# Loads of stored low parts moved to another queue, tile twiddles copied three at a time, operand sums woven in more tightly

## The chip, the core and the metric

The kernel runs on one core of a Trainium2 chip. A core has five engines with an instruction queue each: TensorE (PE, matrix products; PEld is its weight load), VectorE (DVE), ScalarE (ACT), GpSimd (POOL) and SyncE (SP). In this kernel SP and POOL mostly issue DMAs. The metric is device time in microseconds (us), the median over runs. Before the change it is 1392.01 us, over three runs from 1389.22 to 1394.37.

## The reference

The output mixes two branches of the same input `x` (2048 tokens of 576 features) with a gate per token:

```
g = sigmoid((x * gate_w).sum(-1, keepdims=True))
a = irfft2(rfft2(x) * (w_r + 1j * w_i))            # spectral branch, over (2048, 576)
b = (gelu(x @ w_gate) * (x @ w_up)) @ w_down        # 576 -> 4608 -> 576
return g * a + (1 - g) * b
```

All of it is in float32.

## The kernel before

**The dense branch sets TensorE's order.** The 4608 hidden features are 36 tiles of 128 (`j`), the tokens two halves of 1024 (`p`), each of two blocks of 512 (`tb`). A float32 operand is split into a high part of type fp32r and the low rest, and a product is three matmuls: high by high, low by high, high by low. The weights of `j` lie in `gu[j % 3]` (gate and up) and `dn[j % 4]` (down), as `[:, 0]` high and `[:, 1]` low, made from the loaded `raws`. `chain` runs one gate or up product (lines 761 to 768), `hidden` a gate and an up chain and the product of the two, `down_mm` (line 821) the down product. A step `n` of the main loop is two `hidden` calls and four downs of the step before. Its downs are scaled by ScalarE into one of four tiles `stg` (line 846) and added to a DRAM tensor `yd` by an accumulating DMA from POOL's queue (line 834).

**Low parts are kept.** In the first token half (`p` = 0) VectorE subtracts the low parts, and for the first eight `j` they are also stored to DRAM tensors `lo`. In the second half, `lower` (line 730) loads these eight back instead of computing them: `gu<-lo` of 640 KB and `dn<-lo` of 288 KB, both by line 733 in SP's queue. From there on (`products`) seven products per pair of tiles replace eight, for which `operands` and `last_operand` make sums of parts of `x`.

**The spectral branch lies beside it.** It is a mixed-radix transform on VectorE and ScalarE: rows (`forward_rows`), tiles of columns (`first_tiles`, `columns`, `last_tiles`), then back (`inverse_rows`). `columns` also uses TensorE for 64-point products (`product`, line 274, six matmuls per pair of columns) on high and low operands in `colm`: `xh`, `xl` before the filter, `yh`, `yl` after it, where the low one is VectorE's line 267. Corner values move between halves of the partitions by small DMAs in SP's queue (`cns<-til`, `til<-cns`).

**What sets the order.** All instructions are written out in one order by hand. TensorE's chains call `gap()` some 800 times; in each gap the spectral generator gives its next instructions while a credit (VectorE time against TensorE time, `RATE`) is above zero, and `yield None` ends a gap. `columns` has a side generator `beside`, which runs the butterflies and the twiddles of the tiles. Each engine's queue runs in order, so an instruction that waits holds up all behind it on its engine.

**Twiddles.** A tile twiddle turns three complex units. For each, ScalarE copies the unit scaled by a sine into a scratch tile (line 113), and two VectorE instructions combine it in place (lines 127 and 129); for a quarter turn ScalarE does the combination alone (lines 124, 125). `_twiddles` runs the copies `ahead` units in front, which in `beside` is one, with two scratch tiles; the third copy waits until the first scratch is read.

Of the kernel before, what the change touches and what calls it, by code (L numbers as in the profile page):

```python
# [12 lines left out]
AF = mybir.ActivationFunctionType  # L13
# [90 lines left out]
def _twiddles(eng, act, unit, real, imag, places, tmps, sgn, cost):  # L104

    todo = list(places)
    ahead = min(2, len(tmps) - 1)

    def scaled(i):
        if i < len(todo):  # L110
            at, n = todo[i]
            s = 1.0 if n == 4 else sgn * math.sin(math.pi * n / 8)
            act.activation(tmps[i % len(tmps)][0], unit(*at), AF.Copy, scale=s)

    yield None
    for i in range(ahead):
        scaled(i)
    yield None
    for i, (at, n) in enumerate(todo):
        scaled(i + ahead)  # L120
        c, (_, tr, ti) = math.cos(math.pi * n / 8), tmps[i % len(tmps)]
        xr, xi = real(*at), imag(*at)
        if n == 4:
            act.activation(xr, ti, AF.Copy, scale=-float(sgn))
            act.activation(xi, tr, AF.Copy, scale=float(sgn))
            continue
        eng.scalar_tensor_tensor(xr, xr, c, ti, op0=ALU.mult, op1=ALU.subtract)
        yield cost
        eng.scalar_tensor_tensor(xi, xi, c, tr, op0=ALU.mult, op1=ALU.add)
        yield cost  # L130


def _block_of_token():
# [25 lines left out]
def _build(nc, tc, a):  # L159
    with ExitStack() as ctx:  # L160
# [69 lines left out]
        def columns():  # L230
# [62 lines left out]
            def beside():  # L293

                more = gates()
                tmps = [flat[:, SW * i:SW * (i + 1)] for i in (1, 2)]
                for d in range(1, 4):
                    yield from tile_twiddles(d, TAKEN, -1, tmps)
                    yield from four(d, TAKEN, sp, -1)
                    made[0] = d  # L300
                for d in range(3):
                    while gone[0] < (4 * d + 5) * STEP + 5:
                        yield next(more, None)
                    yield from four(d, range(4), sp, 1)
                yield from more
                for k in (1, 2):
                    yield from tile_twiddles(k, LEFT, 1, tmps)
# [19 lines left out]
            for kb in range(18):  # L327
                on, was = kb < 16, 1 <= kb < 17
                if kb < 16:
                    z, (w0, w1) = two(Z[kb]), ww[kb % 2]  # L330
                    zr, zi = z[:, 0], z[:, 1]

                def filter_start():
                    vec.tensor_tensor(zi, v[0][:, :NK], zr, ALU.subtract)
                    vec.tensor_tensor(zr, v[0][:, :NK], zr, ALU.add)

                def swap():
                    act.activation(vs2[0:64], z[64:128], AF.Copy, scale=-1.0)
                    copy(vs2[64:128], z[0:64])

                def filter_end():
                    vec.tensor_tensor(z, z, two(vs), ALU.add)
                    vec.tensor_tensor(vs2[:, 0], zr, zi, ALU.add)
                    vec.tensor_tensor(vs2[:, 1], zr, zi, ALU.subtract)

                for g in range(STEP):
                    if g == 0:
                        while kb % 4 == 2 and kb < 14 and made[0] < kb // 4 + 1:
                            credit[0] -= next(side[0])
                        if on:  # L350
                            v = product(0, kb, xh, xl)
                            load_ww(kb + 1)
                            corner(kb + 2, 0, False)
                        if was:
                            copy(yh, vs)
                    elif g == 1:
                        if on:
                            copy(zr, v[1][:, :NK])
                        if kb + 1 < 16:
                            copy(xh2, two(Z[kb + 1]))  # L360
                        corner(kb - 2, 2, True)
                    elif g == 2:
                        if on:
                            filter_start()
                        if was:
                            low(yl, vs, yh)
                    elif g == 3:
                        if on:
                            swap()
                            corner(kb + 2, 0, True)  # L370
                        if kb + 1 < 16:
                            low(xl2, two(Z[kb + 1]), xh2)
                    elif g == 4:
                        if was:
                            w = product(1, kb - 1, yh, yl)
                            for c in range(2):
                                copy(two(Z[kb - 1])[:, c], w[c][:, :NK])
                        if on:
                            vec.tensor_tensor(z, z, two(w0), ALU.mult)
                            vec.tensor_tensor(vs, vs, w1, ALU.mult)  # L380
                    elif g == 5:
                        if on:
                            filter_end()
                        if was:
                            corner(kb - 1, 2, False)
                    if kb == 17 and g > 4:
                        break
                    credit[0] -= 5.45 / STEP if on else 0.0
                    gone[0] = kb * STEP + g
                    yield None  # L390
# [22 lines left out]

        def tile_twiddles(k, at, sgn, tmps):

            tmps = [(x, x[:, 0:NK], x[:, NK:]) for x in tmps]
            places = [((k, at[o]), o * k) for o in range(1, 4)]
            yield from _twiddles(vec, act, lambda d, e: T[:, d, e], lambda d, e: T[:, d, e, re],
                                 lambda d, e: T[:, d, e, im], places, tmps, sgn, 0.5)

        def last_tiles():

            rows = rows_tile()
            sp = rows[:, 0:4 * SW].rearrange("p (e k) -> p e k", e=4)
            yield from tile_twiddles(3, LEFT, 1, [rows[:, SW * i:SW * (i + 1)] for i in range(4, 8)])
            yield None
            yield from _butterfly(vec, lambda i: T[:, i], lambda i: T[:, i, :, re], lambda i: T[:, i, :, im],
                                  range(4), sp, 1, (2.6, 1.35))
# [132 lines left out]

        def woven(main, other):

            n, free = 0, 0
            for v in main:
                yield v
                n += 1
                if n % 2 == 0 and reloaded[0] and count[0] > free:
                    w = next(other, 0.0)
                    if w is None:  # L570
                        free = count[0]
# [158 lines left out]
        def lower(key, g, r, cost):  # L730
            j, i = key[1], key[0] == "dn"
            if NT <= j < NT + 2 * FIRST:
                nc.sync.dma_start(f(g[:, 1]), lows[j - NT][i])
                return

            def run():
# [574 lines left out]
```

## Time and profile before

| | before |
|---|---|
| median of three runs | 1392.01 us |
| the profiled execution's own time | 1387.69 us |
| its span, first to last instruction | 1385.8 us |
| mean granted TensorE clock | 0.998 |
| TensorE busy | 1366.2 us, 99% |
| VectorE busy | 1119.8 us, 81% |
| ScalarE busy | 703.8 us, 51% |
| GpSimd busy | 266.2 us, 19% |

The page divides the span by engines, lists which group of instructions waited for what, and follows a chain of waits back from the end. `gu<-lo` reads "written `gu`, read `lo`"; L762 is line 762. A number in brackets behind an instruction is the time that its engine was idle before it, and what ended that. TensorE works throughout, so the stretches in which it is idle are the ones that matter.

### The profile page before, as it was taken

The page shows a single profiled execution, that of the slowest core. Times are in us where ns is not written, and L with a number is a line of the kernel's source. Part 1 is how long each engine was busy: PE and PEld are TensorE (multiplying, and loading weights), DVE is VectorE, ACT ScalarE, POOL GpSimd, SP SyncE. Part 2 cuts the span into 40 slices and gives each one's busy share as a digit, 9 for nine tenths or more (in the row PEclk, how much of TensorE's full clock was granted, in tenths as well). Part 3 has the DMA queues.
Part 4 walks back from the last instruction along what each step waited for, and adds up shares of the span by engine and source line. Part 5 has one row for each costly group of instructions (what it writes and reads, how often), then busy time and mean ns, then how long its engine had stood idle before and what let it go on. Part 6 is the DMA issues. An engine that isn't in the chain of part 4 may idle for free.

```text
span 1385.8 us, 20125 instructions
## 1 busy us (share of the span) xinstructions
PE 1366.2 (99%) x7490; PEld 1206.0 (87%) x7490; DVE 1119.8 (81%) x1649; ACT 703.8 (51%) x1095; POOL 266.2 (19%) x326
## 2 busy tenths in 40 slices
PE   9999999999999999999998999999999999999998
PEld 7888888888888888888887888888888888888887
DVE  6989999998877876999979873587777777777776
ACT  5553434355656665444464549445555555555552
POOL 0021111121222211111141023212111121111110
PEclk9999999999999999999999999999999999999999
DMA  9577765668899996556789588767667667776776
GB/s 341 198 179 153 180 116 97 123 117 185 213 272 260 247 235 121 99 112 124 148 185 253 197 171 189 141 128 131 130 129 130 130 130 131 127 129 130 131 154 172
DMA packets 102226, 226.65 MB, mean 164 GB/s; under 512 B 12400, under 2 KB 22640, under 8 KB 101744
## 3 DMA queue, kind: packets, MB, share of 16 engines
q0 software_dynamic: 45248, 92.56, 44.0%
q1 hardware_dynamic: 56880, 132.81, 30.2%
q8 instruction: 59, 0.97, 0.3%
q14 instruction: 39, 0.32, 0.1%
HBM read 118.56 MB, written 99.61 MB: 157 GB/s over the span
## 4 chain that ended last, share of the span: by engine, by line
PE 58%; DMA 1%; DVE 1%; ACT 0%; issue 0%; SPq 0%; DVEq 0%; ACTq 0%
PE pdn L821 20%; PE pgu L1016 4%; PE pgu L1018 4%; PE pgu L1017 4%; PE px L1016 3%; PE px L1018 3%; PE px L1017 3%; PE pgu L762 2%; PE pgu L763 2%; PE pgu L761 2%; PE px L761 2%; PE px L763 2%; PE px L762 2%; PE pgu L1019 2%; PE px L1019 1%; DMA gu<-lo 1%
## 5 line engine op out<-in xcount | busy, mean ns | idle before, releaser
L834 POOL DMA_DIRECT2D yd<-stg x264 | 230.1, 872 | 1028.3 <-ACT stg L846 975.3
L846 ACT ACTIVATE stg<-pdn,omg 128x576 f32<-128x576 f32 x272 | 201.9, 742 | 380.2 <-PE pdn L821 282.1
L821 PEld LDWEIGHTS pdn<-dn,hb 128*128 128x128 f32 x2760 | 382.0, 188 | 11.6 <-DVE raws L875 0.5
L821 PE MATMUL pdn<-dn,hb 128*128 128x288 f32 x2760 | 389.9, 295 | 0.2 <-DVE raws L875 0.2
L762 PE MATMUL pgu<-xhi,gu 128*128 128x512 f32 x440 | 172.5, 392 | 4.2 <-DMA gu<-lo 3.9
L761 PE MATMUL pgu<-xhi,gu 128*128 128x512 f32 x440 | 172.6, 392 | 1.1 <-ACT gl L799 1.1
L763 PE MATMUL pgu<-xlo,gu 128*128 128x512 f32 x440 | 172.1, 391 | 0.0
L213 ACT ACTIVATE gu<-raws 128x1280 fp32r<-128x1280 f32 (+3 forms) x84 | 86.4, 1029 | 38.8 <-PE px L767 28.3
L762 PEld LDWEIGHTS pgu<-xhi,gu 128*128 128x128 f32 x440 | 82.9, 189 | 19.7 <-DMA gu<-lo 4.4
L761 PE MATMUL px<-xhi,gu 128*128 128x512 f32 x256 | 100.0, 390 | 0.0
L763 PE MATMUL px<-xlo,gu 128*128 128x512 f32 x256 | 99.8, 390 | 0.0
L762 PE MATMUL px<-xhi,gu 128*128 128x512 f32 x256 | 99.7, 389 | 0.0
L763 PEld LDWEIGHTS pgu<-xlo,gu 128*128 128x128 f32 x440 | 83.0, 189 | 18.1
L761 PEld LDWEIGHTS pgu<-xhi,gu 128*128 128x128 f32 x440 | 83.0, 189 | 16.3 <-ACT gl L799 1.5
L821 PEld LDWEIGHTS pdn<-dn,gu 128*128 128x128 f32 x672 | 92.2, 188 | 2.1
L821 PE MATMUL pdn<-dn,gu 128*128 128x288 f32 x672 | 93.5, 295 | 0.0
L807 DVE TENSOR_TENSOR hb<-gl,hb 128x512 fp32r<-128x512 f32 x88 | 60.4, 687 | 38.0 <-ACT hb L213 37.9
L799 ACT ACTIVATE gl<-pgu 128x512 f32<-128x512 f32 x55 | 32.8, 596 | 92.3 <-PE pgu L768 85.8
L1034 DVE TENSOR_TENSOR xraw<-xraw 128x512 f32<-128x512 f32 x56 | 38.8, 693 | 31.2 <-ACT xraw L1042 30.7
L1051 DVE TENSOR_TENSOR gl<-gl,pgu 128x512 f32<-128x512 f32 x56 | 38.3, 684 | 27.8 <-PE pgu L1019 27.8
L763 PEld LDWEIGHTS px<-xlo,gu 128*128 128x128 f32 x256 | 48.1, 188 | 10.4
L213 ACT ACTIVATE hb<-gl 128x512 fp32r<-128x512 f32 x88 | 54.9, 624 | 3.3 <-DVE gl L803 3.3
(220 smaller groups left out, 2659.7 us busy)
## 6 DMA issues: line engine op xcount, KB each, us to landing
yd<-stg POOLq DMA_DIRECT2D x264, 288.0 KB, 5.1
raws<-wgu SPq DMA_DIRECT2D x42, 640.0 KB, 5.5
raws<-wd SPq DMA_DIRECT2D x72, 288.0 KB, 3.1
quads<-ws SPq DMA_DIRECT2D x24, 384.0 KB, 4.5
colm<-col POOLq DMA_DIRECT2D x32, 256.0 KB, 6.3
raws<-ws SPq DMA_DIRECT2D x21, 384.0 KB, 4.3
lo<-gu SPq DMA_DIRECT2D x8, 640.0 KB, 4.5
gu<-lo SPq DMA_DIRECT2D x8, 640.0 KB, 6.1
```

The costliest lines, as they stand in the source:

```text
L213: act.activation(o, i, AF.Copy)
L761: pe.matmul(ps, w[:, 0, k, c], xhi[tb][:, k], start=k == 0, stop=False)
L762: pe.matmul(ps, w[:, 1, k, c], xhi[tb][:, k], start=False, stop=False)
L763: pe.matmul(ps, w[:, 0, k, c], xlo[tb][:, k], start=False, stop=False)
L807: vec.tensor_tensor(h[:, 1], g, f(h[:, 0]), ALU.subtract)
L821: pe.matmul(ps[half], h[:, l, c], d[:, q, half * HD:(half + 1) * HD], start=part == 0 and n == 0, stop=part == 1 and n == 2)
L834: pl.dma_start(yd[u], o, accum_op=ALU.add)
L846: put(u, lambda o: act.activation(o.rearrange("p (c k) -> p c k", c=2), v[:, :, 0:HD], AF.Copy, scale=omg[:, u:u + 1]), i == 0)
L1016: pe.matmul(ps, hi[:, c], xh[:, t], start=t == 0, stop=False)
L1017: pe.matmul(ps, lo[:, c], xh[:, t], start=False, stop=False)
L1018: pe.matmul(ps, hi[:, c], xl[:, t], start=False, stop=False)
L1019: pe.matmul(ps, w[:, 512 + P * s:512 + P * (s + 1)], xt, start=False, stop=True)
```

## The change

The loads of the eight kept low parts go from SP's queue to POOL's (`lower`). Tile twiddles get a function of their own, `_three_twiddles`: it makes all three scaled copies in one gap, into three scratch tiles, ends two gaps, and then gives the VectorE instructions. `beside` gets its third scratch tile from a free part of `tmp`; `last_tiles` uses three of its four. The row twiddles keep `_twiddles`. A catch-up loop in `columns` accepts that the side generator ends a gap. `woven`, which gave one instruction of `operands` after every second row instruction, gives one after each.

```diff
+def _three_twiddles(eng, act, units, powers, tmps, sgn, cost):
+    yield None
+    for (x, _, _), n, (t, _, _) in zip(units, powers, tmps):
+        act.activation(t, x, AF.Copy, scale=1.0 if n == 4 else sgn * math.sin(math.pi * n / 8))
+    yield None
+    yield None
+    for (_, xr, xi), n, (_, tr, ti) in zip(units, powers, tmps):
+        c = math.cos(math.pi * n / 8)
+        for o, t, op, s in ((xr, ti, ALU.subtract, -float(sgn)), (xi, tr, ALU.add, float(sgn))):
+            if n == 4:
+                act.activation(o, t, AF.Copy, scale=s)
+            else:
+                eng.scalar_tensor_tensor(o, o, c, t, op0=ALU.mult, op1=op)
+                yield cost
...
-                tmps = [flat[:, SW * i:SW * (i + 1)] for i in (1, 2)]
+                tmps = [flat[:, SW * i:SW * (i + 1)] for i in (1, 2)] + [tmp[:, 3 * SW:4 * SW]]
...
-                            credit[0] -= next(side[0])
+                            credit[0] -= next(side[0]) or 0.0
...
         def tile_twiddles(k, at, sgn, tmps):
-            tmps = [(x, x[:, 0:NK], x[:, NK:]) for x in tmps]
-            places = [((k, at[o]), o * k) for o in range(1, 4)]
-            yield from _twiddles(vec, act, lambda d, e: T[:, d, e], lambda d, e: T[:, d, e, re],
-                                 lambda d, e: T[:, d, e, im], places, tmps, sgn, 0.5)
+            parts = [(x, x[:, 0:NK], x[:, NK:]) for x in tmps]
+            units = [(T[:, k, at[o]], T[:, k, at[o], re], T[:, k, at[o], im]) for o in range(1, 4)]
+            yield from _three_twiddles(vec, act, units, [o * k for o in range(1, 4)], parts, sgn, 0.5)
...
-            yield from tile_twiddles(3, LEFT, 1, [rows[:, SW * i:SW * (i + 1)] for i in range(4, 8)])
+            yield from tile_twiddles(3, LEFT, 1, [rows[:, SW * i:SW * (i + 1)] for i in range(4, 7)])
...
         def woven(main, other):
-            n, free = 0, 0
+            free = 0
             for v in main:
                 yield v
-                n += 1
-                if n % 2 == 0 and reloaded[0] and count[0] > free:
+                if reloaded[0] and count[0] > free:
                     w = next(other, 0.0)
...
             if NT <= j < NT + 2 * FIRST:
-                nc.sync.dma_start(f(g[:, 1]), lows[j - NT][i])
+                pl.dma_start(f(g[:, 1]), lows[j - NT][i])
                 return
```

The change adds lines, so line numbers of the changed kernel below are 15 to 17 higher: 733 becomes 748, 267 becomes 284, 607 becomes 622, 803 becomes 818.

The first place is the load of the low parts of `gu_71` for `j` = 37, the second tile of the second token half. Before, it stood in SP's queue, where `xt` is the input that is loaded again for the second half:

```order
L1177 DMA xraw<-xt 128x512 x2
L711 DMA raws<-wgu 128x1280
L712 DMA raws<-wd 128x576
L1177 DMA xraw<-xt 128x512 x2
L733 DMA gu_71<-lo_1280_115 128x1280
L1177 DMA xraw<-xt 128x512
```

Now it stands in POOL's queue, between the additions of the finished first-half spectral tiles (`yd<-til`):

```order
L622 DMA yd_99<-til 128x576
L748 DMA dn_73<-lo_576_114 128x576
L622 DMA yd_100<-til 128x576
L622 DMA yd_101<-til 128x576
L622 DMA yd_102<-til 128x576
L622 DMA yd_103<-til 128x576
L748 DMA gu_71<-lo_1280_115 128x1280
L622 DMA yd_104<-til 128x576
```

The load no longer stands behind four input loads and two weight loads, but behind seven of the eight accumulating DMAs of POOL.

The second place is VectorE at the start of `columns`, where the second tile is twiddled (L127, L129 before, L146 now) and the first low operand `xl` is made (L267 before, L284 now, `colm<-til,colm`). Before:

```order
L100 TENSOR_TENSOR til<-xraw,til 128x580 x2
L127 SCALAR_TENSOR_TENSOR til<-til,xraw 128x290
L129 SCALAR_TENSOR_TENSOR til<-til,xraw 128x290
L127 SCALAR_TENSOR_TENSOR til<-til,xraw 128x290
L129 SCALAR_TENSOR_TENSOR til<-til,xraw 128x290
L92 TENSOR_TENSOR xraw<-til 128x580
L92 TENSOR_TENSOR til<-til 128x580
L807 TENSOR_TENSOR hb_78<-gl_82,hb_78 128x512
L737 TENSOR_TENSOR dn_75<-raws,dn_75 128x576
L267 TENSOR_TENSOR colm<-til,colm 128x580
```

Now:

```order
L100 TENSOR_TENSOR til<-xraw,til 128x580 x2
L822 TENSOR_TENSOR hb_78<-gl_82,hb_78 128x512
L752 TENSOR_TENSOR dn_75<-raws,dn_75 128x576
L284 TENSOR_TENSOR colm<-til,colm 128x580
L146 SCALAR_TENSOR_TENSOR til<-til,xraw 128x290 x2
L146 SCALAR_TENSOR_TENSOR til<-til,tmp 128x290 x2
```

The low operand has moved ahead of the four twiddle instructions and of the two butterfly instructions behind them.

The third place is VectorE at the end of `columns`, where the last low operand `yl` is made (`colm<-tmp,colm`) while the last tile is twiddled. Before:

```order
L344 TENSOR_TENSOR tmp<-til 128x290
L803 TENSOR_TENSOR gl_82<-gl_82,pgu 128x512
L127 SCALAR_TENSOR_TENSOR til<-til,xraw 128x290
L129 SCALAR_TENSOR_TENSOR til<-til,xraw 128x290
L127 SCALAR_TENSOR_TENSOR til<-til,xraw 128x290
L129 SCALAR_TENSOR_TENSOR til<-til,xraw 128x290
L267 TENSOR_TENSOR colm<-tmp,colm 128x580
```

Now:

```order
L361 TENSOR_TENSOR tmp<-til 128x290
L818 TENSOR_TENSOR gl_82<-gl_82,pgu 128x512
L284 TENSOR_TENSOR colm<-tmp,colm 128x580
L146 SCALAR_TENSOR_TENSOR til<-til,xraw 128x290 x2
L146 SCALAR_TENSOR_TENSOR til<-til,tmp 128x290 x2
```

Here too the low operand has passed the four twiddle instructions.

## The prediction

> **What bounds the kernel now.** I read the page's busy times first.
>
> ```profile
> PE 1366.2 (99%) x7490; PEld 1206.0 (87%) x7490; DVE 1119.8 (81%) x1649; ACT 703.8 (51%) x1095; POOL 266.2 (19%) x326
> ```
>
> TensorE is busy for 1366.2 of the span's 1385.8 us, and the change leaves its matmuls as they are. So only its idle time can be won, 19.6 us with the head and the tail of the program. The view of waits, TensorE's part, says for what it stood (total, times, longest, in us):
>
> ```profile
> PE px L274 <- DVE colm L267: 4.0, 2, 2.3
> PE pgu L762 <- DMA gu<-lo: 3.9, 1, 3.9
> PE px L274 <- issue: 1.5, 2, 0.9
> PE pgu L1135 <- DVE gate L1131: 1.5, 1, 1.5
> PE pgu L761 <- ACT gl L799: 1.1, 1, 1.1
> PE px L780 <- DVE xhi L1141: 0.8, 1, 0.8
> PE px L274 <- ACT til L213: 0.7, 1, 0.7
> ```
>
> Rows four and six are the program's start, which the change does not touch. The others lie in `columns` (L274, and the 1.1 of L761), 7.3 us together, and at one load of a kept low part, 3.9. The timeline of TensorE shows that this one costs more than its wait:
>
> ```profile
> 731.21 0.39 PE L768 MATMUL px<-xtl,gu 128*128 128x512 f32 x1
> 731.44 0.39 PE L761 MATMUL pgu<-xhi,gu 128*128 128x512 f32 x1
> 735.76 0.79 PE L762 MATMUL pgu<-xhi,gu 128*128 128x512 f32 x1 [3.93 <-DMA gu<-lo]
> 736.35 0.63 PE L763 MATMUL pgu<-xlo,gu 128*128 128x512 f32 x1
> ...
> 739.17 0.40 PE L761 MATMUL pgu<-xhi,gu 128*128 128x512 f32 x1
> ```
>
> Matmuls begin 0.23 us apart (731.21 to 731.44), but after the wait they take 0.63 instead of 0.39. The one at 739.17 is the ninth after that of 731.44, due at 731.44 + 9 x 0.23 = 733.51. The event costs 5.7 us, 3.9 of waiting and 1.8 of slow matmuls behind it.
>
> **Part one, the kept low parts.** Why is that load late? SP's timeline before it, and POOL's at the same time:
>
> ```profile
> 712.42 2.34 SPq L1177 DMA_DIRECT2D xraw<-xt  x2
> 714.81 1.21 SPq L711 DMA_DIRECT2D raws<-wgu  x1
> 716.07 0.93 SPq L712 DMA_DIRECT2D raws<-wd  x1
> 717.09 0.99 SPq L1177 DMA_DIRECT2D xraw<-xt  x2
> 718.17 0.51 SPq L733 DMA_DIRECT2D gu<-lo  x1
> ```
>
> ```profile
> 714.25 0.87 POOL L607 DMA_DIRECT2D yd<-til  x1 [1.11 <-DMA yd<-stg]
> 716.90 0.87 POOL L607 DMA_DIRECT2D yd<-til  x1 [1.79 <-DMA yd<-stg]
> ```
>
> SP issues it at 718.17, behind six loads, and its queue then shares the DMA engines with POOL's additions. It lands 17.5 us later, the longest of all (least, median, most of the sixteen transfers between `gu` and `lo`; and POOL's row for `yd<-til`, whose last number is the median to landing):
>
> ```profile
> DMA to landing us min/median/max: 3.5/5.5/17.5
> ```
>
> ```profile
> yd<-til POOLq DMA_DIRECT2D x8, 288.0 KB, 12.5
> ```
>
> In POOL's queue the load follows the `yd<-til` of 714.25, so it is issued at 714.25 + 0.87 + 0.87 = 716.0. It must be there at 731.44 + 0.23 = 731.67. The nearest landing time is the neighbours' 12.5 in the same queue and stretch, which gives 728.5; I add 1.5 for its greater size (352 KB more, at the rate of the transfers of 718 to 736 below, 4.96 MB in 18 us, is 1.3): 730.0, in time with 1.7 to spare. By the bounds it lands at 719.5 (3.5 us) or at 733.5 (17.5 us), where 1.8 us of waiting stay. I take the middle: **-5.7 us**, with ends at -5.7 and -3.9. If it came as late as now, nothing would be won; that is a rival below.
>
> [...]
>
> The other fifteen loads were not waited for. They cost POOL 16 x 0.87 = 13.9 us of issuing, and POOL is 19% busy. Who waits behind them on POOL is an addition from `stg`, and behind that ScalarE's scaling, if one of the four tiles is not free; a tile is used again a step of four downs later, 19.1 us by the rows below, so a transfer may take that long, and the rows have at most 12.5 to 17.5. The accumulations gain 2 to 3 us by the loads in their queue, so I cost this at nothing; with the cover gone it is 1 us at the one crowded place. SP loses sixteen instructions and reaches the next input and weight loads earlier. I cost that at nothing too: no wait of TensorE is on them.
>
> **Part two, the tile twiddles.** VectorE's timeline at three places in `columns`:
>
> ```profile
> 328.58 0.46 DVE L127 SCALAR_TENSOR_TENSOR til<-til,xraw 128x290 f32<-128x290 f32 x1 [3.55 <-ACT xraw L113]
> ...
> 333.72 0.76 DVE L267 TENSOR_TENSOR colm<-til,colm 128x580 fp32r<-128x580 f32 x1
> ...
> 351.94 0.46 DVE L127 SCALAR_TENSOR_TENSOR til<-til,xraw 128x290 f32<-128x290 f32 x1 [1.71 <-ACT xraw L113]
> ...
> 533.85 0.46 DVE L127 SCALAR_TENSOR_TENSOR til<-til,xraw 128x290 f32<-128x290 f32 x1 [0.95 <-ACT xraw L113]
> 534.22 0.46 DVE L129 SCALAR_TENSOR_TENSOR til<-til,xraw 128x290 f32<-128x290 f32 x1
> 534.59 0.76 DVE L267 TENSOR_TENSOR colm<-tmp,colm 128x580 fp32r<-128x580 f32 x1
> ```
>
> At 328.58 the twiddle had waited 3.55 us for its scaled copy, and the low operand that TensorE needs stood eight instructions behind it, so that TensorE waited 1.7 of its 4.0. In the changed order the low operand stands ahead of the twiddles, needs none of them, and can move up by as much as the 3.55 and the time of the six instructions that it passes (0.46 x 4, and two butterflies of 0.76 by the same size as L267's): some 6.9. TensorE asks one gap earlier. A step is twelve gaps, and its downs in the chain of waits come 562.82 - 543.71 = 19.1 us apart, so a gap is 1.6:
>
> ```profile
> 543.71 3.18 PE pdn L821 x24
> 550.09 3.18 PE pdn L821 x24
> 562.82 3.18 PE pdn L821 x24
> ```
>
> The 1.7 and the 1.6 are both covered. At 534.59 it is the same with the last low operand, where TensorE waited 2.3. There ScalarE's copy was ready early:
>
> ```profile
> 530.77 0.69 ACT L213 ACTIVATE colm<-tmp 128x580 fp32r<-128x580 f32 x1 [3.07 <-DVE tmp L344]
> ```
>
> so the low operand may start at 531.46, over 3 us sooner. Both waits go: **-4.0 us**, with an end at -1.7 if one returns. At 351.94 the waits for copies held the read of TensorE's first result, and its next product waited 0.6 behind "issue"; with the copies two gaps ahead it goes: **-0.6**, with 0 as the other end.
>
> The instructions themselves cost nothing new: three copies, four to six VectorE instructions and two for a quarter turn are the same per tile, under a TensorE that is busy. The copies are now always a burst of three ahead of ScalarE's other work, some 2 us by the 0.69 of the row above. The side generator takes a gap more per tile, so that `columns` runs one or two gaps earlier in its middle and meets the old place at its end.
>
> What stays is 0.9 + 1.1 + 0.7 = 2.7 us of waits that no edit names, and all their neighbours have moved against TensorE by a gap. They may go (-2.7) or double (+2.7) and I see no row to choose by; since fresh orders also find fresh waits I put **+1.5** for them.
>
> **Part three, the operand sums.** The same instructions, earlier and closer; their last user is TensorE's seven products, and the page has VectorE (tenths in 40 slices of 34.6 us) far from full just before:
>
> ```profile
> DVE  6989999998877876999979873587777777777776
> ```
>
> Slices 25 and 26 (3 and 5 tenths) lie at the end of the sums. They cover a change of order by some gaps: **0**. Should the sums crowd `hb`'s low parts in the two full steps ahead, a VectorE instruction of 0.7 us per `hidden`, four times, is 2.8.
>
> **Sum.** -5.7 - 4.0 - 0.6 + 1.5 = -8.8 us against the profiled execution's 1387.7, that is 1378.9. The runs shown have a median 4.3 above that execution; with the same offset the median is **1383.2 us**, 0.63% less than 1392.0. I count 0.5%, 7.0 us, as the least that a measurement of this kernel can tell from no change.
>
> **Rivals.** *The load stays late.* For: POOL's queue is the crowded one at this place, and the load queues behind additions in it. The DMA part of the page, asked for 718 to 736 us alone, gives packets, MB and busy share:
>
> ```profile
> q0 software_dynamic: 1069, 2.19, 64.7%
> q1 hardware_dynamic: 1074, 2.77, 43.4%
> ```
>
> As many packets of POOL's queue (q0) as of SP's (q1), though POOL had the more work: a load behind a backlog there gets half the turns. Against: 2.2 us earlier issue, and q1 no longer has it. [...] Then -4.6 alone holds, with the +1.5 left out as in that case nothing downstream moves: 1387.4.
>
> *The waits only move.* In `columns` new ones of like size take the place of the named ones, since the order around all of them is new: -5.7 alone, 1386.3. For it speaks that the 2.7 have four causes; against it that the two long waits have a named cause each.
>
> *Corner values come late: slower.* The changed order puts `til<-cns` of four columns a gap closer behind loads of `raws` in SP's queue. ScalarE's copy waits for them ahead of `gl`:
>
> ```profile
> 400.52 0.69 ACT L213 ACTIVATE colm<-til 128x580 fp32r<-128x580 f32 x1 [4.33 <-DMA til<-cns]
> ```
>
> This was the wait of 1.1 for `gl`: 3.2 of 4.33 were covered. If four such copies came 3.2 us later than here, each would cost TensorE 4.3 and, as after the 3.9, 1.8 of slow matmuls: 24 us in all, 1392.0 - 8.8 + 24 = 1407. It eats the gain up from 1.1 us each (4 x (1.1 + 1.1) = 8.8). Against it: the loads ahead of them are as large as before, and one such wait in all of `columns` reached TensorE.
>
> *Better than forecast.* All of 5.7 and 7.3 goes: 1392.0 - 13.0 = 1379.0.
>
> **Chances.** Forecast 0.50, load late 0.17, moved waits 0.17, better 0.10, slower 0.06. Below 1385.0 lie the better case and four fifths of the forecast, with a little of the two middle ones: faster 0.55. Above 1399.0 lies most of the last: slower 0.05. The rest, 0.40, is within. The range reaches from 1377, the better case and its spread over runs, to 1390, the late load with the 2.7 doubled: two in ten stay outside.
>
> **What would show it.** No wait of TensorE for `gu<-lo`, no stretch of slow matmuls near 735 and a granted clock of 1.0 there; no wait L274 <- DVE L284; L113's and L146's waits for copies gone from VectorE. Wrong would be: a landing of `gu<-lo` from POOL above 15.7 us; waits for ScalarE's `gl` or for px above 2.7 in all; ScalarE waiting for `til<-cns`; a wait for `stg`.

## The result, and the profile after

The changed kernel takes **1374.67 us** (median of six runs, 1373.86 to 1379.04). The kernel before takes 1390.01 in the same comparison (1387.25 to 1394.37). The ratio is 0.989, with an interval from 0.987 to 0.9911: 15.3 us less. The forecast was 1383.2, with a range from 1377 to 1390, so the direction was right and the gain was 1.7 times the 8.8 us that I had worked out.

There are two profiled executions of the changed kernel. The first is the longest of its runs, with 1379.04 us of its own. The second, from a later comparison, has 1372.66. Its busy times, and then TensorE's part of its waits (total, times, longest, in us):

```profile
PE 1362.4 (99%) x7490; PEld 1205.3 (88%) x7490; DVE 1119.1 (82%) x1649; ACT 703.8 (51%) x1095; POOL 275.2 (20%) x342
```

```profile
PE pgu L1150 <- DVE gate L1146: 1.5, 1, 1.5
PE px L795 <- ACT xhi L230: 0.8, 1, 0.8
PE px L795 <- DVE xhi L1156: 0.7, 1, 0.7
PE pdn L836 <- DVE hb L822: 0.2, 1, 0.2
PE pdn L836 <- DVE raws L890: 0.2, 1, 0.2
PE pgu L777 <- DVE gu L1165: 0.2, 1, 0.2
```

All that stays over 0.3 us is the program's start. Not one wait is left in `columns`, where 7.3 us were named before, and none for `gu<-lo`. The first profile has one wait in `columns`, at 442 us, where the kernel before had none:

```profile
PE pgu L776 <- ACT gl L814: 3.0, 1, 3.0
PE pgu L1150 <- DVE gate L1146: 1.5, 1, 1.5
PE pdn L836 <- ACT stg L861: 1.1, 2, 0.8
```

**A finer account than the list of waits.** The list shows idle time. It does not show matmuls that run slowly. So I took all 7490 matmul starts of a trace. For each I took the distance to the next start, less the usual distance for its shape (0.227 us for 512 columns, some 0.13 for 288 or 290), and summed this loss over two stretches: `columns` (300 to 545 us) and the region of the first kept loads (700 to 755 us). A stretch of `columns` without any wait has 1.9 by this sum. Each row stands for one profiled execution with its own time:

| kernel | own time | loss in `columns` | loss at the loads | own time less both |
|---|---|---|---|---|
| before, first profile | 1387.69 | 12.3 | 6.0 | 1369.4 |
| before, second profile | 1392.32 | 14.3 | 7.8 | 1370.2 |
| operand sums only | 1388.94 | 12.7 | 6.1 | 1370.1 |
| load queue only | 1385.29 | 13.7 | 1.2 | 1370.4 |
| twiddles only | 1379.21 | 5.3 | 3.9 | 1370.0 |
| changed, first profile | 1379.04 | 6.7 | 2.5 | 1369.8 |
| changed, second profile | 1372.66 | 1.9 | 1.1 | 1369.7 |

The last column is the same within 1 us, so these two stretches hold the whole difference. The loads gave 4.9 us (6.0 to 1.1), near the 5.7 of the forecast. `columns` gave 10.4 (12.3 to 1.9), where the forecast had 3.1. That is the miss.

### The profile page after: what moved, and what is told of

The parts are those of the page before. It is cut to its first block, busy times and chain, and to the rows that moved or that the text cites. A ratio compares the mean times of both kernels' runs of the same rounds, so it can differ in the third digit from the quotient of the medians.

```text
span 1377.2 us, 20147 instructions
## 1 busy us (share of the span) xinstructions
PE 1365.4 (99%) x7490; PEld 1207.9 (88%) x7490; DVE 1119.4 (81%) x1649; ACT 703.7 (51%) x1095; POOL 275.2 (20%) x342
## 4 chain that ended last, share of the span: by engine, by line
PE 93%; DMA 3%; DVE 2%; issue 1%; ACT 1%; SPq 0%; DVEq 0%; ACTq 0%
PE pdn L836 31%; PE pgu L776 7%; PE pgu L778 7%; PE pgu L777 7%; PE px L776 4%; PE px L778 4%; PE px L777 4%; PE pgu L1031 4%; PE pgu L1033 4%; PE pgu L1032 4%; PE px L1031 3%; PE px L1033 3%; PE px L1032 3%; PE pgu L1034 2%; PE px L291 2%; PE pgu L782 2%
## 5 line engine op out<-in xcount | busy, mean ns | idle before, releaser
L778 PEld LDWEIGHTS px<-xlo,gu 128*128 128x128 f32 x256 | 48.1, 188 | 10.4
```

Of the source, the lines that this page charges most:

```text
L778: pe.matmul(ps, w[:, 0, k, c], xlo[tb][:, k], start=False, stop=False)
```

## The experiments

### The kernel before, profiled again

No edit. The question was where the +4.3 us belong that I carried over from the profiled execution to the median.

> The kernel before, unchanged, with a profile of its own and the granted clock of every run. Two theories for the +4.3 us that I carried over from its profiled execution (1387.7) to its runs (median 1390.0). Theory O (the offset belongs to the stalls that the change removes): the runs spread over some 5 to 7 us (1387 to 1394), and the slower ones have a lower granted clock, about 0.001 for each 1.4 us, or a longer wait for gu<-lo or px in the new profile. Rival F (the offset is a fixed part of any run without the profiler): runs lie within 2 us of each other, all 3 to 5 us above the profiled execution.

Measured: 1389.88 us (twelve runs, 1386.50 to 1393.05), ratio 1.0003 (0.9992 to 1.0015). 23 more runs of the same kernel beside it have a median of 1389.39 (1387.02 to 1392.47). So the offset to the first profile is 1.7, not 4.3; the three runs shown happened to be high. This second profiled execution lies 2.4 above the median of its own twelve runs, so such an offset is the place of one draw in the spread. Rival F falls, since the runs are not within 2 us of each other. The spread goes with the clock, as theory O has it: of these 35 runs the four with a granted clock of 0.996 have a median of 1392.0, the twelve with 0.998 one of 1388.2. This second profile, at 1392.32, shows where such time goes:

```profile
534.15 0.43 PE L274 MATMUL px<-colm 128*128 128x290 f32 x2
536.92 1.34 PE L274 MATMUL px<-colm 128*128 128x290 f32 x4 [2.34 <-DVE colm L267]
538.05 0.63 PE L761 MATMUL pgu<-xhi,gu 128*128 128x512 f32 x1
```

It is the same wait of 2.3 us as in the first profile, but behind it the matmuls run at half speed (0.63 instead of 0.39), which they did not do there. The last section has what the records show of this. The loss in `columns` is 2.0 larger than in the first profile: some 1.4 of that is this half speed, 1.3 a longer wait for `gl` near 400 us (2.4 in place of 1.1), and 0.7 is saved at 462 us, where nothing waits this time.

### Only the load's queue

```diff
-                nc.sync.dma_start(f(g[:, 1]), lows[j - NT][i])
+                pl.dma_start(f(g[:, 1]), lows[j - NT][i])
```

> Only the loads of the kept low parts move to POOL's queue; twiddles and operand sums as before. By the prediction's sum: -5.7 us against the kernel before, no wait for gu<-lo, waits in columns unchanged at some 7.3 us. Theory O (typical runs of the kernel before lose more at this load than its profiled one did): -8 to -10 us, and the runs lie closer together. Rival N (the gain beyond the forecast comes from the twiddles): -5 to -6 us with the old spread of several us. Rival L (the load stays late): 0 to -2 us.

Measured: 1383.80 us (1383.45 to 1387.58), against 1389.39 for the kernel before: -5.6, ratio 0.9968 (0.9955 to 0.998). That is near the prediction's -5.7, and not theory O's -8 to -10; the ratio, for which the mean of the runs counts, gives -4.5 us, with an interval from -2.8 to -6.3. The wait for `gu<-lo` is gone and the loss there falls to 1.2. The waits in `columns` are not the same as expected, though: 9.4 us in place of 7.3, since those for `gl` (2.4) and `til` (1.6) are longer. POOL's timeline, the landing of this one load (least, median, most of the stretch that holds it alone), and TensorE's matmul that needs it:

```profile
712.05 4.93 POOL L607 DMA_DIRECT2D yd<-til  x4
716.66 0.89 POOL L733 DMA_DIRECT2D gu<-lo  x1
```

```profile
DMA to landing us min/median/max: 16.9/16.9/16.9
```

```profile
734.60 0.39 PE L762 MATMUL pgu<-xhi,gu 128*128 128x512 f32 x1
```

It lands at 716.66 + 16.9 = 733.6, only 1.0 us before it is needed. The move bought an earlier issue, not a faster transfer: 16.9 us to landing, beside 17.5 in SP's queue. What counts is the lead, from the issue to the matmul that needs the load. It is 17.9 us here and was 13.5 in the first profile of the kernel before. It is 17.0 to 18.9 in nine profiles with the load in POOL's queue (the one with graded stalls left out), and 12.8 to 14.1 in the four with SP's. SP gave it less, since in that queue the load stood behind input loads, and one of these had to wait for VectorE (SP's waits from 704 to 720 us of the kernel before; total, times, longest):

```profile
SPq L1177 <- DVE xlo L702: 8.5, 2, 6.9
```

### Only the tile twiddles

The edit is `_three_twiddles` with its two callers; the loads stay in SP's queue and `woven` stays as before.

> Only the tile twiddles change (three copies in one gap, two gaps ahead); loads stay in SP's queue, operand sums every second row instruction. By the prediction's sum: -4.6 us for the named waits, +1.5 for fresh ones, so -3.1, and the wait for gu<-lo with its slow matmuls stays. Theory U (the unnamed 2.7 us of waits in columns go too): -7.3. Theory O: -5 to -7 with the old spread of several us, since the late load stays. Rival N: -9 or more.

Measured: 1378.76 us (1377.51 to 1379.58), -10.6, ratio 0.9924 (0.9911 to 0.9937). Rival N had -9 or more. So the gain beyond the forecast comes from this part, as that rival had it. In its profile `columns` lost 5.3 us, against 12.3 to 14.3 in the profiles with the old twiddles; no wait for `colm` is left, and one for `gl` of 2.3 is.

### Only the operand sums

```diff
-                n += 1
-                if n % 2 == 0 and reloaded[0] and count[0] > free:
+                if reloaded[0] and count[0] > free:
```

> Only the operand sums are woven in after every row instruction instead of every second. By the prediction: 0 (within 1 us). A rival, that the sums were late for the first seven-product tile or held up hb's low parts: -1 to -3 us, and some wait of TensorE behind L780 or L821 gone from the profile; or +2.8 if they crowd hb's low parts.

Measured: 1389.07 us (1386.43 to 1395.63) against 1389.39, ratio 1.0001 (0.9989 to 1.0013). It does nothing that can be told apart (the interval is -1.5 to +1.8 us), as forecast. The three parts alone sum to -5.6 - 10.6 - 0.3 = -16.5, near the -15.3 of all together.

### The changed kernel, second profile

> The changed kernel, unchanged, with a new profile. Its first profiled execution (1379.0) was the longest of its six, the others stand at 1374 to 1375. Theory G (half-speed clock comes in fixed windows of 3.413 us, and only after a window in which TensorE was idle for about 2.0 us or more: all six profiles so far have it after 2011, 2384, 2629, 2866 and 3413 ns of idle, and not after 1923 or less): runs at 1373.5 to 1375 with clock 0.999 to 1.000 have no wait over 2 us; runs near 1379 have the wait for gl at 441 us of about 3 us and one dip (1.7 us). The new profile shows either both or neither. Rival: the 1379 is noise of that one execution, and the wait for gl stands at 3.0 us in every run.

Measured: 1374.08 us (1372.66 to 1374.39), ratio 0.9887 (0.9874 to 0.9901). The waits of this profile are shown above: none over 2 us, a granted clock of 1.000, and no half-speed stretch before the end. That agrees with theory G: both are missing here, both are there in the 1379.04. ScalarE's timeline at the place, first in the 1379.04 and then here:

```profile
444.08 0.69 ACT L230 ACTIVATE colm<-til 128x580 fp32r<-128x580 f32 x1 [6.21 <-DMA til<-cns]
444.68 0.58 ACT L814 ACTIVATE gl<-pgu 128x512 f32<-128x512 f32 x1
```

```profile
439.81 0.69 ACT L230 ACTIVATE colm<-til 128x580 fp32r<-128x580 f32 x1 [2.04 <-DMA til<-cns]
440.40 0.58 ACT L814 ACTIVATE gl<-pgu 128x512 f32<-128x512 f32 x1
```

ScalarE's copy waits for the corner values ahead of `gl`. A wait of 2.04 is covered; 6.21 leaves 2.97 for TensorE. That is the mechanism of my slower rival, seen in one place of one execution. It cost 6.7 - 1.9 = 4.8 us there: the wait of 2.97, and 1.6 by the matmuls that begin in the half-speed window behind it (446.09 to 449.51 us, clock 0.50), with 0.2 of lost overlap (explained below).

### Copies in a burst, without the ended gap

The change has two sides: the three copies come together, and one more gap ends between them and their use. The next two kernels separate them.

```diff
     yield None
-    yield None
     for (_, xr, xi), n, (_, tr, ti) in zip(units, powers, tmps):
```

> The changed kernel with one of the two ended gaps taken out between the three copies and the VectorE instructions of a tile twiddle: copies still in one burst and three scratch tiles, but the low operand stands behind the twiddle at both ends of columns, as before. Theory P (place: the low operand's place in VectorE's order made the two long waits; my prediction's step): waits for colm near 333 and 533 us are back with some 3 to 4 us in sum, time 1378 to 1382. Rival C (copies: what counted was that VectorE waited for copies one by one; with the burst it waits once): the waits stay away or are under 1.5 us in sum, time 1374 to 1376.5.

Measured: 1380.37 us (1377.56 to 1383.37), ratio 0.9935 (0.9921 to 0.9949). TensorE's waits in `columns` are back:

```profile
PE pgu L775 <- ACT gl L813: 1.8, 1, 1.8
...
PE px L290 <- DVE colm L283: 1.4, 2, 1.2
PE px L290 <- ACT til L229: 0.9, 1, 0.9
PE px L290 <- issue: 0.9, 1, 0.9
```

The two for `colm` are 1.4 in sum, where theory P had 3 to 4: the burst alone shortens the one near 533 from 2.3 to 0.3. By its waits rival C, with under 1.5 in sum, is just met. The time is in P's range all the same, since waits that neither theory named (`gl`, `til`, "issue") are back too. The burst without the gap is worth 1383.8 - 1380.4 = 3.4 us beside the moved load, by the medians of two comparisons on two chips, and 4.6 by their ratios.

### One copy ahead, with the ended gap

```diff
     for i in range(ahead):
         scaled(i)
     yield None
+    yield None
     for i, (at, n) in enumerate(todo):
```

The edit is in `_twiddles`, for the calls of `tile_twiddles` only, which use it again with its old scratch tiles.

> The changed kernel with the old tile twiddle (one copy ahead, two scratch tiles, the next copy made at the twiddle before), and only one more ended gap between the first copy and its use: the low operand stands ahead of the twiddle at both ends of columns, as in the change. Theory P: the two long waits stay away, time 1374 to 1377. Rival C: VectorE's waits for copies come back (10 us in sum), TensorE waits for colm again by 3 to 4 us, time 1378 to 1382.

Measured: 1373.13 us (1373.09 to 1375.64), ratio 0.9888 (0.9873 to 0.9903). That is the whole gain without the third scratch tile and without the burst. The low operand stands where it does in the change; VectorE waits for copies one by one as before, and TensorE does not notice. VectorE's groups for `columns` have this row (times, busy, mean ns of one, idle before), and TensorE's list has no wait there:

```profile
L129 DVE SCALAR_TENSOR_TENSOR til<-til,xraw 128x290 f32<-128x290 f32 x13 | 5.9, 457 | 9.5 <-ACT xraw L113 9.5
```

```profile
PE pgu L1153 <- DVE gate L1149: 1.5, 1, 1.5
PE px L798 <- DVE xhi L1159: 0.6, 1, 0.6
PE pdn L839 <- DVE hb L825: 0.3, 1, 0.3
```

So 9.5 us of VectorE's waiting cost nothing. Rival C falls.

What the gap does can be counted in the traces. For each of the 32 products of `columns` I counted TensorE's other matmuls ahead of it. Without the gap (before, burst with one gap) the numbers begin with 1757, 1830, 1853, 1867, 1922; with it (change, twiddles only, this kernel) with 1749, 1818, 1847, 1861, 1905. 29 of the 32 products have moved ahead against the dense chain, by 3 to 29 matmuls; the last three stand where they stood.

### Corner values ahead of the filter loads

```diff
-                            load_ww(kb + 1)
                             corner(kb + 2, 0, False)
+                            load_ww(kb + 1)
```

> The changed kernel with two statements swapped in columns: the first leg of the corner values (72.5 KB) goes into SP's queue ahead of the two filter loads (290 KB each) of the next pair instead of behind them. Theory W (the late corner values at 441 us come from the filter loads ahead of them in the same queue): the first leg lands 2 us or more earlier, the wait for gl at 441 us falls under 1 us, no dip, time 1371 to 1373.5. Rival E (the DMA engines are full there whatever the order): the wait stays at 2 to 3 us, time 1374 to 1375, or more if the filter loads become late.

Measured: 1374.07 us (1373.24 to 1375.00), against 1374.08 for the change on the same chip. It buys nothing that can be told apart: that is rival E's time. ScalarE's copy near 438 has no wait at all in this profile, but in the change's second profile the wait was covered as well. Whether the swap keeps away the rare late case is not decided by four runs.

### The gap at the first twiddle only, at the last ones only

```diff
-                    yield from tile_twiddles(d, TAKEN, -1, tmps)
+                    yield from tile_twiddles(d, TAKEN, -1, tmps, int(d == 1))
...
-                    yield from tile_twiddles(k, LEFT, 1, tmps)
+                    yield from tile_twiddles(k, LEFT, 1, tmps, 0)
```

The last argument is the number of additional ended gaps. In the second kernel it is 0 for every `d`, and 1 for the twiddles at the end.

> The changed kernel with the second ended gap kept only in the first tile twiddle of columns and taken out of the other twiddles. With no such gap the time was 1380.4, with all of them 1374.1, so 6.3 us are to be divided. Theory P (each low operand has its own place): only the wait at 333 us goes (1.2 to 1.9 us with its refill), those from 353 to 533 us stay; time 1378 to 1379.5. Rival S (shift: one ended gap moves all of columns by a gap against TensorE's dense chain, and every wait from there on goes with it, until the place where columns meets its old order): waits from 333 to 510 us go, that near 533 stays; time 1374.5 to 1376.5.

> The changed kernel with the second ended gap kept only in the tile twiddles at the end of columns and in the last tiles. Theory P: the wait for colm near 533 us goes, those at 333 to 510 us and the wait for gl at 400 us stay; time 1378 to 1380. Rival S: the same here, since the shift begins only at 520 us or so; what tells the two apart is the run with the first gap only. If the time is under 1376 both are wrong.

Measured: 1378.47 us (1376.70 to 1380.01) with the first gap only, 1379.94 (1377.99 to 1383.86) with the last only; ratios 0.9924 (0.9904 to 0.9944) and 0.9936 (0.9913 to 0.9958).

With the first gap only, all products stand as in the change. The waits at 400, 501 and 509 us, which the burst with one gap still had, are gone: that is rival S. The time is not S's but in P's range, because the wait at 333 is not gone, but longer, 2.2 us, with a half-speed window behind it (the two matmuls there take 0.81 us, the two ahead of the wait 0.43). VectorE's timeline there, and TensorE's:

```profile
328.73 0.83 DVE L147 SCALAR_TENSOR_TENSOR til<-til,xraw 128x290 f32<-128x290 f32 x2 [2.81 <-ACT xraw L137]
329.88 0.83 DVE L147 SCALAR_TENSOR_TENSOR til<-til,tmp 128x290 f32<-128x290 f32 x2 [0.32 <-ACT tmp L137]
...
332.58 0.76 DVE L285 TENSOR_TENSOR colm<-til,colm 128x580 fp32r<-128x580 f32 x1
```

```profile
333.39 0.81 PE L292 MATMUL px<-colm 128*128 128x290 f32 x2 [2.21 <-DVE colm L285]
```

The low operand again stands behind the twiddles of the next tile, which wait 2.81 for their copies, while TensorE, one gap ahead, asks earlier. In the change the same low operand is computed before those twiddles:

```profile
328.79 0.76 DVE L284 TENSOR_TENSOR colm<-til,colm 128x580 fp32r<-128x580 f32 x1
329.47 0.83 DVE L146 SCALAR_TENSOR_TENSOR til<-til,xraw 128x290 f32<-128x290 f32 x2
```

So P is right for the head of `columns`, and S for its middle. At the tail both expected the wait near 533 to stay. It is gone, and the burst with one gap had already brought it down to 0.3, so this run does not tell the two apart there. With the last gaps only, `columns` loses 12.0 us in its profile, and the waits of the burst with one gap stay at 333, 400, 504 and 512 us (1.2, 3.0, 0.7 and 0.9), as both theories had it.

### One size changed: one gap more

`tile_twiddles` in `beside` with 2 as its last argument, so three ended gaps.

> The changed kernel with three ended gaps in place of two between the copies and their use in every tile twiddle of columns: one size changed. If the ended gap gives slack (low operands earlier than TensorE asks for them, and a shift by one gap is as good as by two): 1373 to 1375, no wait in columns. If the order with one gap more is a lucky fit between the two chains: new waits of 2 to 6 us, 1376 to 1380, at other products than before.

Measured: 1375.81 us (1373.21 to 1377.35), ratio 0.9903 (0.9881 to 0.9926): no better, and its interval overlaps with the change's. Its profile has a wait in `columns` at a new place, and one for `stg`:

```profile
PE px L292 <- issue: 1.8, 1, 1.8
PE pdn L837 <- ACT stg L862: 1.7, 1, 1.7
```

This profile is of the second longest of its four runs; two others, with 1373.21 and 1374.30, are as short as the change's. Between the two expectations the runs do not decide.

The third gap did not move `columns` again. Counted as above, 28 of the 32 products stand exactly where they stand in the change; only the first three come earlier, and the last one later. The wait of 1.8 is ahead of one of the 28, the 29th. VectorE's read of the last result (`til<-px`) ends just before that product starts:

```profile
503.74 0.46 DVE L353 TENSOR_TENSOR til<-px,til 128x290 f32<-128x290 f32 x1
```

```profile
504.31 1.43 PE L292 MATMUL px<-colm 128*128 128x290 f32 x6 [1.83 <-issue]
```

In the change's second profile that read ends at 499.75, and the product starts at 501.88 without a wait. So the places of the products do not decide alone. VectorE's order between them does too; that the product waited for this read is inferred from the two times.

### Graded stalls

```diff
-                act.activation(g, pg, AF.Gelu_apprx_tanh)
+                for _ in range(LADDER.get(i, 1)):
+                    act.activation(g, pg, AF.Gelu_apprx_tanh)
```

> The changed kernel, in which ScalarE makes the same gelu 8 to 20 times over (0.58 us each) in ten of the 144 hidden calls, far apart, so that TensorE stalls there by graded lengths, from nothing to some 5 us. Nothing else changes; only the repeats are additional work. Theory G (fixed windows of 3.413 us; half speed in the next window where TensorE was idle for more than some 1.92 to 2.01 us of one): each dip in the record starts a whole number of windows after the first, lasts one window or a whole number of them, and follows windows with more than 1.95 us of idle and no others, so that a stall of 2 to 3 us has a dip or none by where it falls. Rival T (a stall longer than a threshold makes the dip, wherever it lies): dips sort by the length of the stall, with no regard to the windows.

Measured: 1411.05 us (two runs). Its waits for `stg` are nine and 26.2 us in sum. All four half-speed stretches begin a whole number of windows of 3.413 us after the record's first change of the clock (54, 73, 173 and 192 of them) and last one or two windows. The windows ahead of them have 2.15, 3.04, 3.41 and 2.52 us without a matmul. Windows with 1.66 and 1.90 have none behind them. So it went as theory G had it. Rival T falls within this trace, since the shorter of these two waits has half speed behind it, and the longer has none:

```profile
664.78 4.97 PE L838 MATMUL pdn<-dn,hb 128*128 128x288 f32 x24 [2.52 <-ACT stg L863]
...
727.69 3.45 PE L838 MATMUL pdn<-dn,hb 128*128 128x288 f32 x24 [3.13 <-ACT stg L863]
```

The first lies in one window, the second in two, with 1.90 us in the fuller one. The last section shows the same in a pair of other kernels, 2.34 us with and 3.36 without.

## Why the prediction was wrong

**What bounds the kernel:** right. TensorE's idle time in `columns` and at one load was all there was to win, and the account above finds nothing elsewhere.

**The load, -5.7:** right, -5.6 alone. Its landing was mis-sized: I had 12.5 + 1.5 = 14.0 us from issue, the run has 16.9, and 15.7 and 16.2 in the two profiles of the change. The issue was placed right (716.0 forecast, 716.66 measured). It was in time by 1.0 us rather than 1.7, and only because TensorE reached the place 2.9 us later in that execution than in the profile I reckoned with: the lead was 17.9 us, and I had 731.67 - 716.0 = 15.7. The two errors, 2.9 in the landing and 2.2 in the lead, nearly cancel, so luck had a part in the number: a landing of 16.9 with my lead of 15.7 would have left a wait of 1.2. "The load stays late" was nearer than I had it. POOL's additions did not suffer: `yd<-stg` takes 874 ns each, 872 before.

**The two long waits, -4.0:** gone, at the head by the mechanism that I gave: put the low operand behind the twiddles again, and 2.2 us return. At the tail either side of the change is enough by itself (0.3 us is left with the burst alone, none with one copy ahead and the additional gap).

**"Issue", -0.6:** gone, but it did not need copies two gaps ahead: with the burst one gap ahead it is gone too.

**The remaining waits, +1.5: this is the step that failed.** I had the shift itself right ("`columns` runs one or two gaps earlier in its middle and meets the old place at its end"), and what it is worth wrong. I wrote that all the neighbours of these waits "have moved against TensorE by a gap", that they may go or double, and that "since fresh orders also find fresh waits" I put +1.5. The runs have -2.7 for them: all went, by that same shift. And a cost was in no row that I read, so that I put it at nothing:

- Each of these waits cost some 0.16 us more than the list says: two neighbouring matmuls overlap by that much (0.39 us long, begun 0.23 apart), and the wait took the overlap away. The start-to-start distance at the tail wait is 2.48 us over the usual one, for a wait of 2.32. For six waits that is 1.0.
- Three products (at 354, 462 and 510 us) ran some 0.46 us long within their six matmuls, and with a wait of 0.16 at 462 us (a row of 0.2 that I had left out) they make 1.7 together.
- Small losses make up the other 0.4.

So the term for `columns` was -4.0 - 0.6 + 1.5 = -3.1, and in its place the first profile has 4.6 (the named waits) + 2.7 (the unnamed ones) + 3.1 (in no row that I read) = 10.4. Above that come half-speed windows behind the waits, which the first profile had only at the load (735.55 to 738.96 us, clock 0.50), but the second also in `columns` (some 1.4 of its 14.3).

**The offset, +4.3:** failed too. It came from three runs. By 23 runs it is 1.7; for the second profile of the same kernel it would have been below zero; and for the changed kernel the median lies 2.0 above its second profile (1374.67 - 1372.66).

The miss is 1383.2 - 1374.7 = 8.5: 7.3 from `columns` (10.4 less 3.1) and 2.3 from the offset (4.3 less 2.0), less 0.8 at the load (5.7 less 4.9 in the account), with 0.3 unaccounted.

**The operand sums, 0:** right.

**The rivals.** The load stays late, the waits only move: both wrong. (The 2.7 us of waits have three causes by the rows, not the four that I counted for the second.) Corner values late: the mechanism exists, at one place, and clearly in one of the changed kernel's ten runs, for 4.8 us. The twiddles-only kernel, whose `columns` is in the same order, has 2.3 at the same place (442.8 us) in its one profile, so it may be less rare than one in ten. Better than forecast had the right cause (everything in `columns` goes), and still 4.3 too much for the time, because it counted idle rows at their face value and used the same offset. What I named as proof of error appeared: waits for `gl` above 2.7, ScalarE waiting for `til<-cns` and waits for `stg` (1.1 us, where ScalarE had waited 7.4 and 3.2 for the input `xraw<-xt`) in the first profile, and a landing above 15.7 us (16.2) in the second. Yet the forecast was wrong to the other side.

What stays open: why this shift by a gap leaves no wait at all. In the middle of `columns` the waits go with the products' place against the dense chain. But the run with one gap more has a wait with the products in the same places, so VectorE's order has its part, and I give no rule by which the loss of an order could be read ahead of a run.

## What to carry to other kernels

Where two instruction chains are woven by hand or by a credit, one ended gap can move most of what stands behind it (29 of 32 products here, though the next one moved only four): look first at which instructions change their place on the bounding engine, and price every wait in that stretch, not only those whose own neighbours were edited. Sum start-to-start distances of the bounding engine against their usual value, since the whole list of waits leaves out 2.9 of 10.4 us here. Take the offset between a profiled execution and the median from many runs, or leave it out and widen the range.

## What the runs showed of the hardware

**Half speed came in windows of 3.413 us.** In the first profile of the kernel before, the record of the granted clock has 0.50 from 735.545 to 738.958 us, and the first profile of the changed kernel has it from 446.093 to 449.506: 3.413 us each. They begin 730.453 and 436.906 us behind the record's first entry, which is 214 and 128 times 3.4133. At half speed the matmuls of 512 columns begin 0.427 us apart, otherwise 0.227. The records of all fourteen profiles, the ends of the program left out, change only at whole numbers of 3.413 us. There are eleven stretches at half speed. Every one begins behind a window in which TensorE had 2.01 to 3.41 us without a matmul (2.01 in the second profile of the kernel before, 2.63 in the first of the changed kernel, 3.41 in the first of the kernel before), and no window at full speed with 1.92 or less has one behind it. In the graded stalls the stretch from 194.0 us went on for a second window, where the first still had 2.05 us of idle; in the second profile of the kernel before a stretch ended behind a window with 0.32, in the first behind one with 0.21. So the length of a wait does not sort these cases; how much of it fell into one window does. The tail wait of 2.3 us in the second profile of the kernel before, and the same wait in the load-only kernel (columns: window, its length, busy time and instructions of PE, PEld, DVE, ACT and POOL, granted clock, DMA share, GB/s):

```profile
533.20:536.60 3.40, 1.38 (x7) 0.95 (x6) 2.07 (x5) 3.40 (x8) 0.86 (x1) 1.00 0.46 78
536.60:540.00 3.40, 3.08 (x9) 2.70 (x10) 1.62 (x3) 1.83 (x5) 0.86 (x1) 0.50 0.94 244
```

```profile
533.20:536.60 3.40, 2.26 (x11) 1.69 (x9) 1.66 (x4) 3.40 (x7) 0.86 (x1) 1.00 0.34 80
536.60:540.00 3.40, 2.21 (x11) 1.95 (x12) 2.49 (x5) 2.81 (x7) 0.87 (x1) 1.00 0.92 230
```

In the first, 2.0 us of it lie in one window, and the next is at 0.50, which costs some 1.5 us. In the second, the wait lies across the border, 1.1 and 1.2, and the clock stays at 1.00. Even the wait of 3.36 us for `gu<-lo` in the twiddles-only kernel had no half-speed window behind it; it fell into two halves, with 1.70 and 1.65 us of idle:

```profile
723.70:727.10 3.40, 1.70 (x8) 1.08 (x6) 3.37 (x4) 1.32 (x3) 0.00 (x0) 1.00 1.07 301
727.10:730.50 3.40, 1.75 (x8) 1.44 (x9) 2.03 (x4) 0.00 (x0) 0.00 (x0) 1.00 1.08 272
```

The windows lay differently against the program in the two profiles of the kernel before: a window began at 735.545 us in the first and at some 536.6 in the second, and the 198.9 us between are 58.3 windows. In the first, the tail wait lies across a border, with 1.07 and 1.25 us of idle in its two windows, and no half speed follows; in the second it cost some 1.5 us more. An estimate, if all positions are equally likely: for a wait of w between 2 and 3.4 us, and a limit of 1.97 (the middle of 1.92 and 2.01), the share of positions with more than the limit in one window is (3.41 + w - 3.94) / 3.41: 0.52 for 2.3, 0.99 for 3.9 by the same line. That is a likely reason, not shown run by run, for part of the spread of the kernel before over 7 us, and for the changed one's 1372.7 to 1375.1 without its longest run.
